# Hash attention and gated MLP: gaps in the buffers that VectorE reads bits from, and VectorE casts in parts of 7 and 5 stripes

## The chip, the core and the metric

The kernel runs on one core of a Trainium2 chip. Its time is the device time of one execution in microseconds (us), which is a little more than the span from the first to the last instruction in the profile. The engines are named as in the profile: PE is TensorE's matmuls and PEld its weight loads, DVE is VectorE, ACT is ScalarE, POOL is GpSimd and SP is SyncE; a "q" behind a name means the engine's queue. Durations of single instructions are in nanoseconds (ns).

## What is computed

Attention in which a query sees only keys of its own hash bucket, and a gated MLP behind it. Shapes: batch 4, heads 8, sequence 768, head size 64; 6 hash bits; the MLP has 3072 rows, width 512 and inner width 1536.

```python
q_bits = (np.einsum('bhsd,dk->bhsk', q, proj) > 0)      # 6 bits for each token
mask = q_bucket[:, :, :, None] == k_bucket[:, :, None, :]
scores = np.where(mask, scale * q @ k.T, -1e9)
attn = softmax(scores) @ v                               # then heads side by side: x (3072, 512)
g, val = x @ w_gate, x @ w_val
ffn_out = (gelu(g) * val) @ w_out
out = x + sigmoid(x @ w_res) * ffn_out
```

## The kernel before

**Tiles.** The 32 heads go in 16 pairs p (4 pairs for each batch element). For each pair and each side (q, k) the tokens lie in a tile `raw` of 128 partitions by 12 stripes of 64 floats: 6 stripes for each head of the pair. A second tile `nat` (6 of them in a ring, `nat_of`, 128 partitions by 12 stripes of 128 bf16) takes, in each stripe, the 64 values as bf16 (`cast`, L183 to L192), then 6 hash bits as plus or minus one half in columns 64 to 69, then a constant. So the product of a q and a k stripe contains the score and a large bonus for equal bits; a wrong bucket is driven to nothing by the exponential. `nat` is transposed into `aug`, in the first batch element by PE (`turn_pe`, evacuated by `turned`), later by DMA (`turn`).

**Bits.** There are three ways to them.
- `hash_mm`, `hash_tok`, `bits`: DVE transposes blocks of 32 by 32 (`tr`, L201), PE multiplies with the projection, DVE transposes the result back (`hash_tok`, L223) into a tile of 12 stripes of 32 floats, and four instructions (`bits`, L232) compare 32 partitions each with zero and write the bits into `nat`. For pairs 2 and 3 that tile is `ht` in SBUF; for the later batch elements it is `htp` in PSUM.
- `hash_heads`, `tok_heads` (L291), `bits_head` (L298): the same for pair 1, one head at a time, with a tile `hth` of 6 stripes in SBUF. Pair 0 uses `hash_one` and `bits_one`, in PSUM alone.
- `multiply` (L264, POOL), `add_up` (L271, DVE), `bits_val` (L275): for half of the later pairs POOL multiplies the tokens with the projection, DVE adds the products up into `hval` (tile hv, 12 stripes of 6 floats in SBUF), and one instruction on POOL or DVE compares.

**Stages.** `scores` makes two banks of scores with PE and one exponential of 128 x 1024 on ACT (L452); `values` multiplies the exponentials with v (L421); there are 9 such slots to a pair and 36 to a batch element. `finish` (L367, L368) normalizes into `x_tok`. After batch element b, `gate_val` runs the MLP's first half (L477 on PE, Gelu on ACT in L497, product on DVE in L499); its second half (`project`, L511 to L534) is spread between the attention slots of the next batch element.

**Order.** The schedule is manual: each engine executes its instructions in the order of the code. For the first batch element that order is written out by hand in the string ORDER, whose pieces are put up with `put`. The part that matters below reads:

```python
"scores 18, bits 3k, finish 10, vals_s 2, av 15, turn 2k1, ld 6q, evac 2q1, "
"scores 19, bits 3q, av 16, "
"scores 20, load_w 3, vals_a 3, evac 2k1, av 17, av 18, "
"scores 21, av 19, turn 3q0, "
"scores 22, turn 3k0, evac 3q0, "
```

WHO says which engine takes a piece: DVE casts 2k and 3k ("cast 2k", "cast 3k"), ACT casts 3q, POOL most of the others. Bits of a q side are compared on DVE, those of a k side on POOL and DVE by turns. For the later batch elements the tables FIRST and LATER give each piece a slot, and ON_ACT and ON_DVE an engine; `bits_val` is on DVE for two tiles of the second batch element and on POOL otherwise. The SP queue issues the loads and the DMA transposes, in order; POOL's queue issues the loads of the MLP's weights.

Of the kernel before, what the change touches and what calls it, by code (L numbers as in the profile page):

```python
# [9 lines left out]
FP32 = mybir.dt.float32  # L10
BF16 = mybir.dt.bfloat16
AF = mybir.ActivationFunctionType
ALU = mybir.AluOpType
# [4 lines left out]
def kernel(  # L18
# [12 lines left out]
    nc = tc.nc  # L31
    B, H, S, D = q.shape
    NBITS = proj.shape[1]
    DMODEL = H * D
    DFF = moe_w_gate.shape[1]
    P = 128
    KM = DMODEL // P
    KF = DFF // P
    T = S // P
    HP = H // 2  # L40
    NPAIR = B * HP
    HT = 2 * T
# [22 lines left out]
    hv_pool = ctx.enter_context(tc.tile_pool(name="hv", bufs=2))  # L65
    sm_pool = ctx.enter_context(tc.tile_pool(name="sm", bufs=2))
# [6 lines left out]
    raw, rawv, aug, vaug, vsums = {}, {}, {}, {}, {}  # L73
# [95 lines left out]
    for s in range(3):  # L169
        n = KF // 3  # L170
# [8 lines left out]
    def nat_of(x):  # L179
        return nat[(2 * x[0] + x[1]) % NN]  # L180

    def cast(p, side, eng, h0=0, h1=2):
        x = (p, side)  # L183
        scale = (1.0 / C) if side == 0 else 1.0
        sl = slice(h0 * T, h1 * T)
        dst = nat_of(x)[:, sl, 0:D]
        if eng is nc.scalar:
            nc.scalar.activation(dst, raw[x][:, sl], AF.Copy, scale=scale)
        elif side == 0:
            eng.tensor_scalar(dst, raw[x][:, sl], scale, 1.0, op0=ALU.mult, op1=ALU.mult)  # L190
        else:
            eng.tensor_copy(dst, raw[x][:, sl])  # L192

    t32, hsum, htok = {}, {}, {}
    TRING = (0, 1, 2, 0, 1, 2, None, None, 0, 1, None, None, 0, 1)
# [21 lines left out]
    def hash_tok(jobs, psum=False):  # L217
        n = 32 * len(jobs)
        if psum:
            ht = av_ps.tile([P, HT, 32], FP32, tag="av", name="htp")  # L220
        else:
            ht = sm_pool.tile([P, HT, 32], FP32, tag="ht", name="ht")
        nc.vector.transpose(ht[:n].rearrange("p c n -> p (c n)"),  # L223
                            hsum[jobs[0]][:n].rearrange("p c n -> p (c n)"))
        for j, x in enumerate(jobs):
            htok[x] = (ht, j)

    def bits(p, side, engs=(nc.vector,)):
        x = (p, side)
        ht, j = htok.pop(x)  # L230
        for a in range(4):
            engs[a % len(engs)].tensor_scalar(  # L232
                nat_of(x)[32 * a:32 * a + 32, :, D:D + NBITS],
                ht[32 * j:32 * j + 32, :, NBITS * a:NBITS * (a + 1)], 0.0, 0.5,
                op0=ALU.is_gt, op1=ALU.subtract)


# [17 lines left out]
    hval, prod = {}, {}  # L255
# [11 lines left out]

    def add_up(x, t):
        if x not in hval:
            hval[x] = hv_pool.tile([P, HT, NBITS], FP32, tag="hv", name="hv")  # L270
        nc.vector.tensor_reduce(hval[x][:, t:t + 2, :], prod.pop((x, t)),  # L271
                                axis=mybir.AxisListType.X, op=ALU.add)

    def bits_val(x, eng):
        eng.tensor_scalar(nat_of(x)[:, :, D:D + NBITS], hval.pop(x), 0.0, 0.5,  # L275
                                op0=ALU.is_gt, op1=ALU.subtract)


    def hash_heads(p, dh):
# [7 lines left out]
                             start=(dh == 0), stop=(dh == 1), tile_position=(0, 32 * j))  # L287

    def tok_heads(p):
        ht = sm_pool.tile([P, T, 32], FP32, tag="ht", name="hth")  # L290
        nc.vector.transpose(ht.rearrange("p c n -> p (c n)"),  # L291
                            hsum.pop(p).rearrange("p c n -> p (c n)"))
        htok[p] = ht

    def bits_head(p, side, hi, engs):
        j = 2 * hi + side
        for a in range(4):
            engs[a % len(engs)].tensor_scalar(  # L298
                nat_of((p, side))[32 * a:32 * a + 32, hi * T:hi * T + T, D:D + NBITS],
                htok[p][32 * j:32 * j + 32, :, NBITS * a:NBITS * (a + 1)], 0.0, 0.5,  # L300
                op0=ALU.is_gt, op1=ALU.subtract)

    def turn(p, side):
# [336 lines left out]
    def tokens(ps, psum=False):  # L640
        hash_tok([(p, side) for p in ps for side in range(2)], psum)
# [17 lines left out]
    for h in range(2):  # L659
        for e in range(2):  # L660
            x = "0%s%d" % ("qk"[e], h)
            put("tr " + x, lambda e=e, h=h: tr(0, e, h, h + 1))
            put("hash " + x, lambda e=e, h=h: hash_one(0, e, h, av_ps, "av"))
            put("cast " + x, lambda e=e, h=h, x=x: cast(0, e, WHO.get("cast " + x, G), h, h + 1))
            put("bits " + x, lambda e=e, h=h: bits_one(0, e, h))
            if x == "0q1":
                put("turn " + x, lambda: turn_pe(0, 0, 1, "av", av_ps))
            else:
                put("turn " + x, lambda e=e, h=h: turn_pe(0, e, h))
            if e == 0:  # L670
                put("evac " + x + "a", lambda h=h, x=x: turned(0, 0, h, WHO.get("evac " + x + "a", V), 0, 4))
                put("evac " + x + "b", lambda h=h, x=x: turned(0, 0, h, WHO.get("evac " + x + "b", V), 4, T))
            else:
                put("evac " + x + "a", lambda h=h, x=x: turned(0, 1, h, WHO.get("evac " + x + "a", V), 0, 2))
                put("evac " + x + "b", lambda h=h, x=x: turned(0, 1, h, WHO.get("evac " + x + "b", V), 2, T))
# [3 lines left out]
    for p in range(1, HP):  # L679
        for e in range(2):  # L680
            x = "%d%s" % (p, "qk"[e])
            put("tr " + x, lambda p=p, e=e: tr(p, e))
            put("cast " + x, lambda p=p, e=e, x=x: cast(p, e, WHO.get("cast " + x, G)))
            if p == 1:
                for h in range(2):
                    put("bits %s%d" % (x, h), lambda p=p, e=e, h=h, x=x: bits_head(p, e, h, WHO.get("bits %s%d" % (x, h), ((V,), (G, V))[e])))
            else:
                put("bits " + x, lambda p=p, e=e, x=x: bits(p, e, WHO.get("bits " + x, ((V,), (G, V))[e])))
            for h in range(2):
                y = "%s%d" % (x, h)  # L690
                put("turn " + y, lambda p=p, e=e, h=h, y=y: turn_pe(p, e, h, BANK[p][2 * h + e]))
                put("evac " + y, lambda p=p, e=e, h=h, y=y: turned(p, e, h, WHO.get("evac " + y, V)))
    for i in range(2):
        put("hash 1.%d" % i, lambda i=i: hash_heads(1, i))
    put("toks 1", lambda: tok_heads(1))
    for i in range(4):
        put("hash 2.%d" % i, lambda i=i: hashed((2, 3), i, i + 1))
# [17 lines left out]
    for b in range(B - 1):  # L715
        s0, p0 = b * NSLOT, (b + 1) * HP
        xs = [(p0 + i, side) for i in range(2) for side in range(2)]
        ys = [(p0 + 2 + i, side) for i in range(2) for side in range(2)]
        for j, (x, y) in enumerate(zip(xs, ys)):
            if b == 0:  # L720
                for z in (x, y):
                    n = "%d%s" % (z[0], "qk"[z[1]])
                    put("ld " + n, lambda z=z: load(*z))
                n = "%d%s" % (x[0], "qk"[x[1]])
                put("tr " + n, lambda x=x: tr(*x))
            else:
                place(b, "tr x", j, lambda x=x: tr(*x))
                place(b, "ld x", j, lambda x=x: load(*x))
                place(b, "ld y", j, lambda y=y: load(*y))
            place(b, "bits x", j, lambda x=x: bits(*x))  # L730
            place(b, "turn x", j, lambda x=x: turn(*x))
            place(b, "cast x", j, lambda x=x, e=who(b, "x%d" % j): cast(*x, e))
            place(b, "cast y", j, lambda y=y, e=who(b, "y%d" % j): cast(*y, e))
            place(b, "bits y", j, lambda y=y, e=who(b, "b%d" % j): bits_val(y, e))
            place(b, "turn y", j, lambda y=y: turn(*y))
            for t in range(T):
                place(b, "mul y%d" % j, t, lambda y=y, t=t: multiply(y, 2 * t))
                place(b, "add y%d" % j, t, lambda y=y, t=t: add_up(y, 2 * t))
        if b > 0:
            place(b, "hash", 0, lambda p0=p0: hashed((p0, p0 + 1)))  # L740
        place(b, "toks", 0, lambda p0=p0: tokens((p0, p0 + 1), True))
# [101 lines left out]
    for s in range(NSLOT - 1, LAST):  # L843
        p, c = divmod(s, NCH)
# [63 lines left out]
```

## Time and profile before

| | us |
|---|---|
| median of 3 runs | 342.3 |
| lowest and highest | 340.31, 344.82 |
| the profiled execution | 342.28 |
| its span | 340.6 |
| busy: PE, DVE, ACT, POOL | 328.7, 232.1, 221.7, 207.7 |
| first batch element's attention, until the Gelu table is loaded | 0 to 48.0 |
| first half of the MLP for it, until the next scores | to 81.8 |

A line of the timeline or of a list of instructions names the source line, the engine, the operation, the tile written and the tiles read, and the shapes as partitions x elements. In a list of instructions "x12: 185/194/2595" is the count and the shortest, the median and the longest duration in ns. A line of the waits names who waited for whom, and gives the total in us, the number of times and the longest. The granted clock of PE was 0.998 of full speed.

### The profile page before, as it was taken

What the parts mean: (1) busy time and instruction counts of PE and PEld (TensorE: products, weight loads), DVE (VectorE), ACT (ScalarE), POOL (GpSimd) and SP (SyncE); (2) the same over time, 40 slices, a digit from 0 to 9 for tenths busy, and PEclk for the clock granted to TensorE, in tenths of its full rate; (3) what the DMA queues carried; (4) which work ended last, traced back from release to release, by engine and by line L of the source; (5) the groups of instructions that cost most, each with busy time, mean ns of one, the idle gap of its engine ahead of it and who ended that gap; (6) DMA issues with size and microseconds to landing.
All of it is one profiled execution on the core that took longest, in us unless ns stands there. A gap on an engine that the chain in (4) does not pass through costs nothing.

```text
span 340.6 us, 7565 instructions
## 1 busy us (share of the span) xinstructions
PE 328.7 (97%) x2994; PEld 202.6 (60%) x3040; DVE 232.1 (68%) x422; ACT 221.7 (65%) x278; POOL 207.7 (61%) x236
## 2 busy tenths in 40 slices
PE   8997899999999999999999999999999999999995
PEld 5676665555666655565666665666566665566443
DVE  7899867998567877676777876776776344343343
ACT  5997984337999972345999992234999994223120
POOL 4899687899988682579989691579989000000000
PEclk9999999999999999999999999999999999999999
DMA  7989939799968350523996452502553331000012
GB/s 234 376 158 207 268 91 195 141 156 182 315 167 204 89 138 33 92 46 61 245 227 194 100 153 72 94 17 52 117 95 84 80 79 64 0 1 2 31 63 93
DMA packets 69827, 42.70 MB, mean 125 GB/s; under 512 B 47904, under 2 KB 66848, under 8 KB 69792
## 3 DMA queue, kind: packets, MB, share of 16 engines
q1 hardware_dynamic: 63376, 36.97, 43.4%
q0 software_dynamic: 6336, 5.24, 11.0%
q8 instruction: 24, 0.39, 0.5%
q14 instruction: 11, 0.09, 0.1%
q10 hardware_dynamic: 80, 0.00, 0.0%
HBM read 29.56 MB, written 6.29 MB: 105 GB/s over the span
## 4 chain that ended last, share of the span: by engine, by line
PE 88%; DVE 6%; issue 2%; ACT 2%; DMA 2%; DVEq 0%; ACTq 0%
PE sp L477 24%; PE fps L525 17%; PE sp L447 16%; PE av L421 9%; PE gvr L477 6%; PE rps L511 6%; PE gvf L477 3%; DMA x_sb<-x_tok 2%; PE hs L213 2%; ACT e L452 1%; DVE nat L232 1%; DVE hh L499 1%; PE pt L317 1%; DVE nat L135 1%; PE hs L242 1%
## 5 line engine op out<-in xcount | busy, mean ns | idle before, releaser
L264 POOL TENSOR_TENSOR pr<-ld,projt 128x768 f32<-128x768 f32 x72 | 129.8, 1816 | 46.2 <-DVE hv L271 45.1
L452 ACT ACTIVATE e<-sp 128x1024 bf16<-128x1024 f32 x144 | 142.6, 1027 | 8.1 <-PE sp L447 3.9
L447 PE MATMUL sp<-aug,aug 71*128 71x256 bf16 (+1 forms) x384 | 86.1, 325 | 1.6 <-ACT e L452 1.4
L525 PE MATMUL fps<-wo,hh 128*128 128x512 bf16 (+2 forms) x290 | 74.6, 361 | 1.1
L421 PEld LDWEIGHTS <-e 128*128 128x128 bf16 x1152 | 53.0, 97 | 29.1 <-issue 0.3
L271 DVE TENSOR_REDUCE hv<-pr 128x12 f32<-128x768 f32 x72 | 66.9, 936 | 3.3 <-POOL pr L264 3.2
L497 ACT ACTIVATE gt<-sp 128x768 bf16<-128x768 f32 x32 | 26.0, 811 | 55.6 <-PE sp L477 55.6
L421 PE MATMUL av<-va,e 128*128 128x65 bf16 x1152 | 57.7, 193 | 0.1
L499 DVE TENSOR_TENSOR hh<-gt,sp 128x768 bf16<-128x768 bf16 x36 | 34.3, 954 | 31.3 <-PE sp L477 29.6
L477 PE MATMUL sp<-x_sb,wv 128*128 128x256 bf16 (+1 forms) x277 | 52.3, 324 | 0.8 <-DVE hh L499 0.2
L477 PEld LDWEIGHTS <-wv 128*128 128x128 bf16 x384 | 37.5, 98 | 25.3 <-issue 0.7
L477 PEld LDWEIGHTS <-wg 128*128 128x128 bf16 x384 | 37.1, 98 | 25.2 <-issue 0.8
L477 PE MATMUL sp<-x_sb,wg 128*128 128x256 bf16 (+1 forms) x252 | 46.8, 325 | 0.3
L525 PEld LDWEIGHTS <-hh 128*128 128x128 bf16 x312 | 28.5, 97 | 22.1
L447 PEld LDWEIGHTS <-aug 71*128 71x128 bf16 x384 | 29.2, 97 | 12.0 <-issue 3.3
L529 DVE SCALAR_TENSOR_TENSOR fps<-th,fps 128x512 f32<-128x512 f32 (+2 forms) x26 | 17.0, 653 | 21.5 <-PE fps L525 20.1
L497 ACT ACTIVATE gt<-gvr 128x512 bf16<-128x512 f32 x16 | 9.6, 597 | 28.9 <-PE gvr L477 27.2
L511 PE MATMUL rps<-wr,x_sb 128*128 128x512 bf16 x90 | 26.4, 379 | 0.4
L515 ACT ACTIVATE th<-rps 128x512 f32<-128x512 f32 x24 | 14.2, 593 | 15.9 <-PE rps L511 15.6
L477 PE MATMUL gvr<-x_sb,wg 128*128 128x512 bf16 x61 | 20.9, 379 | 0.0
L201 DVE STREAM_TRANSPOSE t<-ld 128x768 f32<-128x768 f32 (+1 forms) x22 | 19.1, 883 | 0.0
L367 DVE RECIPROCAL rec<-av 128x6 f32<-128x6 f32 x32 | 6.2, 192 | 18.6 <-PE av L421 16.8
(83 smaller groups left out, 329.4 us busy)
## 6 DMA issues: line engine op xcount, KB each, us to landing
ldv<-in_v_dram SPq DMA_DIRECT2D x16, 384.0 KB, 5.4
out_dram<-o SPq DMA_DIRECT2D x23, 256.0 KB, 2.2
ld<-in_q_dram SPq DMA_DIRECT2D x15, 384.0 KB, 4.7
ld<-in_k_dram SPq DMA_DIRECT2D x15, 384.0 KB, 5.9
wg<-in_moe_w_gate_dram POOLq DMA_DIRECT2D x4, 384.0 KB, 5.7
wv<-in_moe_w_val_dram POOLq DMA_DIRECT2D x4, 384.0 KB, 6.9
wo<-in_moe_w_out_dram POOLq DMA_DIRECT2D x3, 512.0 KB, 6.8
wr<-in_moe_w_res_dram POOLq DMA_DIRECT2D x1, 512.0 KB, 5.7
```

Source lines behind the costliest of these rows:

```text
L201: nc.vector.transpose(t32[p, side][:, sl].rearrange("p c h n -> p (c h n)"), raw[p, side][:, sl].rearrange("p c d -> p (c d)"))
L264: nc.gpsimd.tensor_tensor(pr, raw[x][:, t:t + 2].unsqueeze(2).to_broadcast([P, 2, NBITS, D]), projt.unsqueeze(1).to_broadcast([P, 2, NBITS ...
L271: nc.vector.tensor_reduce(hval[x][:, t:t + 2, :], prod.pop((x, t)), axis=mybir.AxisListType.X, op=ALU.add)
L421: nc.tensor.matmul(av[p, hi][:, qt, :], e[:, off:off + P], va[:, hi, jt, 0:D + 1], start=first, stop=(p >= HP and jt == T - 1), skip_group ...
L447: nc.tensor.matmul(sp[:, off:off + nq * P], ks[0:KA, hi * T + jt, :], qs[0:KA, hi * T + qt0:hi * T + qt0 + nq, :], start=True, stop=True)
L452: nc.scalar.activation(e, sp, AF.Exp, scale=float(ALPHA))
L477: nc.tensor.matmul(o, w[:, kk, bass.ts(m, P)], xs[:, kk, c0:c1], start=(kk == 0), stop=(kk == KM - 1))
L497: nc.scalar.activation(gt[:, c0:c1], o, AF.Gelu)
L499: nc.vector.tensor_mul(hh[:, m, c0:c1], gt[:, c0:c1], o)
L511: nc.tensor.matmul(rps, x_sb[b][:, kk, t, :], wr[:, kk, :], start=(kk == 0), stop=(kk == KM - 1))
L525: nc.tensor.matmul(fps[:, cs], hh[:, m, bass.ts(t, P)], wo[:, m, cs], start=(m == 0), stop=(m == KF - 1))
L529: nc.vector.scalar_tensor_tensor(fps[:, cs], th[:, cs], 1.0, fps[:, cs], op0=ALU.add, op1=ALU.mult)
```

## The change

The tiles `ht`, `hth` and `hv` get room for one more stripe behind every third of their stripes (12 stripes become three groups of 4 with a gap of one stripe behind each; 6 become three groups of 2), and what writes and reads them uses patterns of three groups. The tile `htp` in PSUM stays as it was. A whole cast of a k side on DVE becomes two instructions, of 7 and of 5 stripes; casts of half a tile, casts on POOL and casts of a q side stay as they were.

```diff
+        elif eng is nc.vector and h1 - h0 == 2:
+            for c in (slice(0, 7), slice(7, HT)):
+                eng.tensor_copy(nat_of(x)[:, c, 0:D], raw[x][:, c])
         else:
             eng.tensor_copy(dst, raw[x][:, sl])
...
+    def gapped(n, w, name):
+        full = sm_pool.tile([P, 3, (n // 3 + 1) * w], FP32, tag=name[:2], name=name)
+        return full[:, :, 0:n // 3 * w]
...
-            ht = sm_pool.tile([P, HT, 32], FP32, tag="ht", name="ht")
-        nc.vector.transpose(ht[:n].rearrange("p c n -> p (c n)"),
-                            hsum[jobs[0]][:n].rearrange("p c n -> p (c n)"))
+            ht = gapped(HT, 32, "ht")
+        nc.vector.transpose(ht[:n].rearrange("p c n -> p (c n)") if psum else ht[:n],
+                            hsum[jobs[0]][:n].rearrange("p c n -> p (c n)") if psum else
+                            hsum[jobs[0]][:n].rearrange("p (u c) n -> p u (c n)", u=3))
...
-                ht[32 * j:32 * j + 32, :, NBITS * a:NBITS * (a + 1)], 0.0, 0.5,
+                ht[rows, :, cols] if len(ht.shape) == 3 and ht.shape[1] == HT else
+                ht[rows].rearrange("p u (c n) -> p u c n", n=32)[:, :, :, cols], 0.0, 0.5,
                 op0=ALU.is_gt, op1=ALU.subtract)
...
-            hval[x] = hv_pool.tile([P, HT, NBITS], FP32, tag="hv", name="hv")
-        nc.vector.tensor_reduce(hval[x][:, t:t + 2, :], prod.pop((x, t)),
+            hval[x] = hv_pool.tile([P, 3, HT // 3 + 1, NBITS], FP32, tag="hv", name="hv")
+        nc.vector.tensor_reduce(hval[x][:, t // 4, t % 4:t % 4 + 2, :], prod.pop((x, t)),
...
-        eng.tensor_scalar(nat_of(x)[:, :, D:D + NBITS], hval.pop(x), 0.0, 0.5,
-                                op0=ALU.is_gt, op1=ALU.subtract)
+        eng.tensor_scalar(nat_of(x)[:, :, D:D + NBITS], hval.pop(x)[:, :, 0:HT // 3], 0.0, 0.5,
+                          op0=ALU.is_gt, op1=ALU.subtract)
...
-        ht = sm_pool.tile([P, T, 32], FP32, tag="ht", name="hth")
-        nc.vector.transpose(ht.rearrange("p c n -> p (c n)"),
-                            hsum.pop(p).rearrange("p c n -> p (c n)"))
+        ht = gapped(T, 32, "hth")
+        nc.vector.transpose(ht, hsum.pop(p).rearrange("p (u c) n -> p u (c n)", u=3))
...
-                htok[p][32 * j:32 * j + 32, :, NBITS * a:NBITS * (a + 1)], 0.0, 0.5,
+                htok[p][32 * j:32 * j + 32].rearrange("p u (c n) -> p u c n", n=32)[
+                    :, :, :, NBITS * a:NBITS * (a + 1)], 0.0, 0.5,
                 op0=ALU.is_gt, op1=ALU.subtract)
```

## The prediction

> **What bounds the kernel now.** I read the engine shares first (PE busy for 328.7 of 340.6 us), then a table of busy time by stage, then the waits of the one stage in which PE is not full. From 45.1 to 315.8 us PE is busy for 267.9 of 270.7 us (the sum of its stage rows), so nothing that VectorE saves there can buy more than 2.8 us. The first 45 us are different:
>
> ```profile
> core 0: us, PE busy (x) PEld busy (x) DVE busy (x) ACT busy (x) POOL busy (x), PEclk, DMA share, GB/s
> 20.00:29.70 9.70, 9.70 (x155) 6.98 (x154) 8.91 (x23) 9.55 (x11) 9.01 (x17) 1.00 0.94 105
> 29.70:33.70 4.00, 1.98 (x36) 1.62 (x32) 3.92 (x6) 2.18 (x3) 3.84 (x9) 1.00 1.16 275
> 33.70:45.10 11.40, 10.16 (x145) 7.24 (x143) 8.61 (x15) 11.03 (x13) 7.90 (x9) 1.00 1.10 269
> 45.10:82.20 37.10, 36.51 (x277) 22.24 (x282) 31.51 (x55) 18.06 (x26) 33.23 (x26) 1.00 0.94 143
> ```
>
> The columns are the stretch, its length, and the busy time of PE, PEld, DVE, ACT and POOL. In the second row PE and ACT both lose about half of 4 us while DVE and POOL are full. ACT, with its exponentials, is what limits this part; its timeline shows one hole and no other between 9.4 and 47.9 us:
>
> ```profile
> 22.95 8.93 ACT L452 ACTIVATE e<-sp 128x1024 bf16<-128x1024 f32 x9
> 34.05 6.66 ACT L452 ACTIVATE e<-sp 128x1024 bf16<-128x1024 f32 x7 [2.17 <-PE sp L447]
> 40.56 0.86 ACT L188 ACTIVATE nat<-ld 128x768 bf16<-128x768 f32 x1
> 41.30 6.65 ACT L452 ACTIVATE e<-sp 128x1024 bf16<-128x1024 f32 x7
> ```
>
> The number in brackets is idle time and who ended it. The waits of 9 to 45 us say why PE was late, and the chain of waits names the instruction:
>
> ```profile
> ACT e L452 <- PE sp L447: 2.2, 1, 2.2
> PE pt L317 <- DVE aug L326: 2.0, 1, 2.0
> PEld L317 <- DVE nat L232: 1.6, 1, 1.6
> ...
> 29.79 2.60 DVE nat L232
> 32.41 0.56 DVE aug L326
> 33.02 0.49 PE pt L317 x6
> ```
>
> One TensorScalar that reads bits from ht took 2.60 us. The list of instructions on nat shows how far that is from its kind:
>
> ```profile
> L232 DVE TENSOR_SCALAR nat<-htp x48: 220/228/238, 54.4 to 235.9; 32x72 bf16<-32x72 f32 x48
> L232 DVE TENSOR_SCALAR nat<-ht x12: 185/194/2595, 24.4 to 29.8; 32x72 bf16<-32x72 f32 x12
> L298 DVE TENSOR_SCALAR nat<-hth x6: 171/175/211, 13.4 to 14.4; 32x36 bf16<-32x36 f32 x6
> L192 DVE CAST nat<-ld x2: 723/1216/1710, 20.3 to 21.4; 128x768 bf16<-128x768 f32 x2
> L275 DVE TENSOR_SCALAR nat<-hv x2: 198/928/1657, 69.1 to 85.0; 128x72 bf16<-128x72 f32 x2
> ```
>
> The three long maxima (2595, 1710, 1657 ns) sit on SBUF-to-SBUF TensorScalars and casts. The same operation from PSUM (htp) never leaves 220 to 238 ns in 48 instructions. While the 2595 ns one ran, POOL went back to back (a weight DMA issue 29.66 to 30.48, a cast to 31.33, a memset to 31.41, an addition to 32.32, next start 32.40), and DVE ended at 32.38, in that gap. The 1657 ns one ran from 69.09 to 70.75, and POOL's two DMA issues from 69.17 to 70.72. So these instructions wait for POOL to leave something that both need. Other DVE work beside POOL does not: the TENSOR_REDUCE of L271 reads SBUF 72 times beside 129.8 us of POOL multiplications and stays within 893 to 955 ns. The short instructions are also faster than their PSUM twins (194 against 228 ns for 72 elements), as if they read two halves at once; I take that second path to be what is fought over.
>
> **The change part by part.** The source in three groups and the destination in twelve stripes no longer divide alike into halves, so I expect the 12 ht, 6 hth and 2 hv instructions on DVE to run on one path, and not to wait.
>
> Bits, added: each ht one goes from 194 to about 228 ns (the htp row), 12 x 34 = 0.41 us; each hth one from 175 to 196 ns (the 36-element row of L250, from PSUM), 6 x 21 = 0.13; the two hv ones from 198 to about 232, 0.07. In all 0.6 us of DVE, at most 4 x 0.034 = 0.14 of it in the critical batch. It is hidden by ACT's queue; without that cover it costs those 0.14 us.
>
> Bits, removed: 2595 - 194 = 2.40 us at 29.79, 0.3 us in the two instructions before it (0.28 and 0.40 where 0.19 is normal), and 1657 - 198 = 1.46 us at 69.09.
>
> Casts: two become four. L201, SBUF to SBUF at 547 ns for 384 and 958 ns for 768 elements, gives 1.07 ns an element and 136 ns fixed, an estimate for one path: 0.62 us for 448 elements and 0.48 us for 320, 1.10 a cast, 2.20 for both, against 2.43 now. If the parts still take two paths, it is (0.38 + 0.31) x 2 = 1.38 plus their waits: none to 0.9 us each, about the mean POOL instruction there (0.65, 0.98, 0.84, 1.06), 1.38 to 4.98. I take 2.20. ACT is full from 9.4 to 31.9 us, so earlier casts buy nothing at the end; later ones cost only beyond the 0.6 us from the bits of 2q (about 25.2) to their PE turn at 25.78. [...]
>
> The transposes into gapped tiles (572 ns once, 384 ns once): between 0 and, by the 599 ns htp row, 0.03 us more each. POOL's own readers of the tiles (463 ns x4, 330 ns x10, 468 ns x10): the nearest bound for an awkward pattern is their own spread, 516, 346 and 482 at most, so 0 to 0.5 us over 24 instructions; POOL idles 45.1 us waiting for L271, so I take zero. The reductions into hv write the same 12 numbers. The change adds no wait and no DMA.
>
> What the end gains: without the wait, the last bits of 3q end at 30.0, the evacuation of 2k1 (0.54) at 30.5. PE finishes its values at 31.01 and goes straight on to the turn of 3q0 instead of waiting to 33.02; scores come at 31.35 and are done by about 31.95; ACT ends its earlier exponentials at 31.88. So ACT's hole shrinks from 2.17 to about 0.1: 2.1 us. ACT has no other hole to 47.95, so all of that reaches the MLP stage. There PE waits 0.24 us at 80.29 for a DVE product, which 1.4 us less DVE work at 69 may remove; I take 0.1 of 0 to 0.24. Late next is ACT itself. Sum: 342.28 - 2.1 - 0.1 = 340.1. The profiled execution (342.28, span 340.6) is at the median of the runs (342.3), so no correction.
>
> **Rivals.**
> The gain is lost to a transfer. The chain goes from a DMA of x_sb (33.69, 5.97 us) to ACT's queue at 39.66. If that landing stayed put, ACT's cast, due at 38.4, would wait 1.3 us and the gain be 0.9 or less, down to none if loads brought forward collide (DMA share 1.10 there): 341.4 to 342.3. Against: the queue's event lasts 17 ns, ACT never idles there, and the DMA starts on a product of DVE that moves forward too.
>
> The change does not do what it says: the bits still use both paths in spite of the gap. Then the wait stays where it is, and the time is 342.3. No row has unequal groups, so only the run can tell.
>
> Slower: the casts keep two paths, and four parts each meet POOL. Now two waits cost about 1.35 us (2.43 less two times 0.54). It decides when the parts' waits exceed 1.35 + 0.6 + 2.2 = 4.15 us together. Two of the longest kind (2.40) and two of 0.9 make 6.6, that is 2.5 us too late: 344.7. For it: POOL is full at 20 to 24 us. Against: single POOL instructions there are only 0.65 to 1.06 us. [...]
>
> More than forecast: the waits at 69 and in the casts also cost PE time that the in-order waits hide, the rest of the 0.59 us that PE loses from 45.1 to 82.2, and the hole at 29.79 was mild against other executions (the runs spread from 340.31 to 344.82): about 338.5.
>
> **How the numbers follow.** Forecast as worked out 0.62 (own range 339.2 to 341.2); lost to a transfer 0.13; nothing changes 0.10; slower 0.06; more 0.09. The predicted time is 340.1. From 338.0 to 342.8 all but the slower case lie inside, with some 0.5 us for the spread of runs. Two per cent is 6.8 us, about what a measurement of this kernel can tell from no change: the waits removed add up to 5.4 us of DVE time, so faster by over 2% needs something that I don't see (0.03); slower by over 2% takes nearly three times the worst cast case (0.03); within 2% is 0.94.
>
> **What would show it.** Right: nat<-ht maximum under 250 ns with its median near 228, nat<-hv on DVE near 232 both times, four casts of about 0.62 and 0.48 us, no hole of ACT near 32 us, PE's turn of 3q0 right behind the values. Wrong: ht medians still 194 with long maxima (the gap does nothing), cast parts of 0.4 us and scattered waits, or a new hole of ACT between 32 and 48 us, above all before L188. A time outside 338 to 342.8 with the hole gone would mean that the stages after 45 us moved for a reason not listed.

## The result and the profile after

| | before | after |
|---|---|---|
| median of 22 executions each, us | 344.0 | 340.4 |
| lowest and highest, us | 340.0, 346.14 | 339.24, 342.44 |
| the profiled execution and its span, us | 342.28, 340.6 | 340.34, 338.6 |

The ratio after to before is 0.9936, 95% interval 0.991 to 0.9962: 0.6% faster, clear of noise and within 2%. Ratios here leave out executions that are over 1.5% above the fastest of the same kernel, and in some sets below that drops many of the kernel before; where it matters, the medians of all executions stand beside them.

The instructions on nat that DVE executes, in the profile after (count, then shortest, median and longest ns):

```profile
L244 DVE TENSOR_SCALAR nat<-htp x48: 220/228/240, 52.7 to 234.1; 32x72 bf16<-32x72 f32 x48
L244 DVE TENSOR_SCALAR nat<-ht x12: 216/220/224, 24.7 to 30.1; 32x72 bf16<-32x72 f32 x12
L310 DVE TENSOR_SCALAR nat<-hth x6: 177/182/183, 13.9 to 14.8; 32x36 bf16<-32x36 f32 x6
L193 DVE CAST nat<-ld x4: 469/522/603, 20.8 to 22.7; 128x448 bf16<-128x448 f32 x2, 128x320 bf16<-128x320 f32 x2
L288 DVE TENSOR_SCALAR nat<-hv x2: 221/224/228, 67.4 to 83.1; 128x72 bf16<-128x72 f32 x2
```

No maximum stands out any more. The ht row has moved up to the row of its PSUM twin (220 against 228 ns), and the parts of a cast took 572 and 603 ns for 448 elements and 469 and 473 for 320, that is 0.80 and 1.02 ns for each element more, against the 1.07 ns that the prediction took for one path. "Two paths" and "one path" stand here and below for the faster and the slower duration of such an instruction (194 against 220 ns for 72 elements); that paths lie behind them is the prediction's reading and no profile shows it. That a long one waits for POOL is inferred as well, from where it ends: in the profile before, one at 32.38 us in POOL's gap from 32.32 to 32.40, and one at 70.75 us, 0.03 us behind two DMA issues of POOL. ACT's timeline of the same profile, from the cast of 3q on:

```profile
22.70 0.84 ACT L188 ACTIVATE nat<-ld 128x768 bf16<-128x768 f32 x1
23.43 15.58 ACT L465 ACTIVATE e<-sp 128x1024 bf16<-128x1024 f32 x16
38.87 0.86 ACT L188 ACTIVATE nat<-ld 128x768 bf16<-128x768 f32 x1
39.60 6.65 ACT L465 ACTIVATE e<-sp 128x1024 bf16<-128x1024 f32 x7
46.27 1.28 ACT L873 ACT_TABLE_LOAD   x1
```

The nine and seven exponentials with a hole of 2.17 us between them are now sixteen in a row. This execution's attention began 0.48 us later (first exponential at 9.90 instead of 9.42), so the Gelu table is loaded 1.70 us earlier by the clock (47.97 to 46.27) and 2.18 us earlier against the start. The span is 2.0 us shorter. In the MLP stage the one wait of PE for a product is still there, 0.34 us where it was 0.24:

```profile
40.70 0.59 PE L460 MATMUL sp<-aug,aug 71*128 71x256 bf16 x3 [0.80 <-ACT e L465]
43.45 0.59 PE L460 MATMUL sp<-aug,aug 71*128 71x256 bf16 x3 [0.23 <-ACT e L465]
78.49 1.46 PE L490 MATMUL sp<-x_sb,wv 128*128 128x512 bf16 x8 [0.34 <-DVE hh L512]
```

The numbers in brackets are PE's idle time before the group. The list of PE's waits in this profile has no other from 27 to 83 us (1.0 us for ACT in two, 0.3 us for DVE in one): the 2.02 us before the turn of 3q0 are gone, and up to the MLP stage ACT is what PE waits for.

### The profile page after: what moved, and what is told of

Read it like the earlier page. It is cut to its first block, busy times and chain, and to the rows that moved or that the text cites. A ratio compares the mean times of both kernels' runs of the same rounds, so it can differ in the third digit from the quotient of the medians.

```text
span 338.6 us, 7613 instructions
## 1 busy us (share of the span) xinstructions
PE 331.4 (98%) x3040; PEld 203.0 (60%) x3040; DVE 228.4 (67%) x424; ACT 221.7 (65%) x278; POOL 206.7 (61%) x236
## 4 chain that ended last, share of the span: by engine, by line
PE 90%; ACT 5%; DVE 3%; issue 1%; DVEq 0%; ACTq 0%
PE sp L490 25%; PE fps L538 18%; PE sp L460 16%; PE av L434 9%; PE gvr L490 7%; PE rps L524 6%; ACT e L465 5%; PE gvf L490 3%; PE hs L222 2%; PE hs L255 1%; DVE nat L135 1%; PE pt L330 1%; DVE hh L512 1%; PE pt L418 0%; DVE hv L284 0%
## 5 line engine op out<-in xcount | busy, mean ns | idle before, releaser
L538 PE MATMUL fps<-wo,hh 128*128 128x512 bf16 (+2 forms) x312 | 79.4, 362 | 0.0
L490 PE MATMUL sp<-x_sb,wv 128*128 128x512 bf16 (+1 forms) x288 | 52.8, 326 | 0.3 <-DVE hh L512 0.3
L490 PE MATMUL sp<-x_sb,wg 128*128 128x512 bf16 (+1 forms) x256 | 47.0, 326 | 0.0
L524 PE MATMUL rps<-wr,x_sb 128*128 128x512 bf16 x96 | 28.1, 379 | 0.0
L490 PE MATMUL gvr<-x_sb,wg 128*128 128x512 bf16 x64 | 21.7, 379 | 0.0
```

The costliest lines, as they stand in the source:

```text
L490: nc.tensor.matmul(o, w[:, kk, bass.ts(m, P)], xs[:, kk, c0:c1], start=(kk == 0), stop=(kk == KM - 1))
L524: nc.tensor.matmul(rps, x_sb[b][:, kk, t, :], wr[:, kk, :], start=(kk == 0), stop=(kk == KM - 1))
L538: nc.tensor.matmul(fps[:, cs], hh[:, m, bass.ts(t, P)], wo[:, m, cs], start=(m == 0), stop=(m == KF - 1))
```

## The experiments

Theory A is the prediction's: the gain is the one wait of the bits of 3q. Against it stand B (the sum of all waits removed on VectorE), C (the gap itself, not the uneven count) and, from what the first runs showed, D (the price of a hole in PE is more than its length). All kernels are timed beside the kernel before on the same chip.

**Only the gaps of ht.** The change without its casts, hth and hv:

```diff
+            ht = gapped(HT, 32, "ht")        # and its transpose and reader; nothing else of the change
```

> Only the tile ht has the gaps; hth, hv and the casts are as before. Theory A (the gain is the one wait of the bits of 3q, which is gone because three groups against twelve stripes do not split over two paths): ratio to the kernel before 0.993 to 0.994, no hole of ACT near 32 us, all twelve ht instructions on DVE between 215 and 225 ns, while the casts still have a wait (one over 1.2 us) and one hv instruction on DVE is still over 1.2 us. Theory B (the gain is the sum of all waits removed, 5 us of VectorE time in several places): this gives less than half of the gain, ratio 0.997 or more.

Measured: 340.55 us (339.69 to 340.92), ratio 0.9919 (0.9885 to 0.9953); before, 343.21 us. The ht instructions are at 216/219/223 ns and ACT has no hole. In the same profile the casts and hv still wait:

```profile
L192 DVE CAST nat<-ld x2: 716/1217/1718, 21.0 to 22.1; 128x768 bf16<-128x768 f32 x2
L285 DVE TENSOR_SCALAR nat<-hv x2: 198/918/1637, 67.6 to 83.5; 128x72 bf16<-128x72 f32 x2
```

So the whole gain comes with ht alone, and waits of 1.4 us at 67 us and 1.2 us at 22 us cost nothing that can be measured. Theory B falls.

**All but the gaps of ht.**

```diff
-            ht = gapped(HT, 32, "ht")
+            ht = sm_pool.tile([P, HT, 32], FP32, tag="ht", name="ht")
```

> The complement: hth and hv have the gaps and the casts are in parts of 7 and 5, but ht is as before. Theory A: the wait of one ht instruction stays (over 1.5 us), ACT keeps a hole of 1.5 to 2.2 us near 32 us, ratio 0.998 to 1.002. Theory B: more than half of the gain is here, ratio 0.995 to 0.997. If the casts in parts only moved VectorE by some 0.3 us against POOL, the ht wait may meet another POOL instruction and be of another length; then ACT's hole goes with it.

Measured: 345.57 us (341.83 to 346.5), ratio 1.0061 (1.0022 to 1.0101). That is 0.6% slower than the kernel before, which no theory had said. The wait is there (2420 ns, in the four of the second line below), and a second one that the profile of before does not have: the two ht instructions at 27.65 us took 1.25 us together (before: 0.40 us, at 27.20 us). Together they make PE's hole 2.55 us where it was 2.02, but the price is larger than this length. DVE's and PE's timelines in this profile, and the stages behind the hole:

```profile
27.65 1.25 DVE L243 TENSOR_SCALAR nat<-ht 32x72 bf16<-32x72 f32 x2
30.17 3.19 DVE L243 TENSOR_SCALAR nat<-ht 32x72 bf16<-32x72 f32 x4
31.05 0.41 PE L433 MATMUL av<-va,e 128*128 128x65 bf16 x8
34.00 0.80 PE L329 MATMUL pt<-ident,nat 128*71 128x128 bf16 x6 [2.55 <-DVE aug L338]
34.60 1.06 PE L459 MATMUL sp<-aug,aug 71*128 71x256 bf16 x3
```

```profile
33.00:35.00 2.00, 1.00 (x8) 1.02 (x9) 1.66 (x6) 0.00 (x0) 1.84 (x5) 0.52 1.19 272
35.00:37.00 2.00, 2.00 (x13) 1.31 (x11) 1.01 (x2) 1.02 (x1) 1.54 (x5) 0.50 1.19 266
37.00:39.00 2.00, 2.00 (x19) 1.45 (x18) 0.73 (x2) 1.02 (x1) 0.14 (x1) 0.50 1.33 188
39.00:41.00 2.00, 2.00 (x31) 1.56 (x30) 1.59 (x4) 1.32 (x2) 2.00 (x2) 0.77 1.19 220
```

The third number from the right is the granted clock of PE. It is at a half behind the hole: 0.52, 0.50, 0.50 and 0.77 over 2 us each are 6.8 us at 0.50 and the rest at 1.00. The same six transposes take 0.80 instead of 0.50 us and three scores 1.06 instead of 0.60, and ACT, which waits for scores, has holes of 3.42, 0.47, 0.91 and 0.50 us instead of one. The page of before shows clock 9 in all its slices: its profiled execution had a hole of 2.02 us and kept the clock.

**Only the casts in parts.**

```diff
+            for c in (slice(0, 7), slice(7, HT)):
+                eng.tensor_copy(nat_of(x)[:, c, 0:D], raw[x][:, c])
```

> The casts of 2k and 3k in parts of 7 and 5 stripes, all tiles without gaps. Theory A: ratio 0.998 to 1.002; the four parts take 0.60 and 0.47 us (one path, no waits), the ht wait and ACT's hole stay. The rival that the casts are what makes VectorE late for the bits of 3q: the ht wait is gone and the ratio is 0.994. The slower case of the prediction (parts on two paths, each waiting): parts of 0.4 us with waits and a ratio over 1.003.

Measured: 345.25 us (340.71 to 346.58), ratio 1.004 (0.9991 to 1.0089). The profiled execution is the odd one out of 12, at 340.71 us. It has no wait over 0.2 us in the ht instructions and the casts (hv still waits, 1637 ns at 67.7 us):

```profile
L235 DVE TENSOR_SCALAR nat<-ht x12: 184/191/356, 24.2 to 29.7; 32x72 bf16<-32x72 f32 x12
L193 DVE CAST nat<-ld x4: 470/523/605, 20.3 to 22.2; 128x448 bf16<-128x448 f32 x2, 128x320 bf16<-128x320 f32 x2
```

So the wait of 3q comes in some executions and not in others. Here the last comparison of 3q started at 29.68, 0.09 us into POOL's weight-DMA issue (29.59), and went through in 191 ns; in the kernel before it started at 29.79, 0.13 us into that issue (29.66), and took 2595. All the other 11 executions lie at 343.67 us or above. The parts run on one path without waits (470 to 605 ns), as expected, but with them the bad meeting seems likelier; that they do it by shifting DVE against POOL is not shown.

**Gaps behind halves instead of thirds.**

```diff
-        full = sm_pool.tile([P, 3, (n // 3 + 1) * w], FP32, tag=name[:2], name=name)
-        return full[:, :, 0:n // 3 * w]
+        full = sm_pool.tile([P, 2, (n // 2 + 1) * w], FP32, tag=name[:2], name=name)
+        return full[:, :, 0:n // 2 * w]
```

> As the changed kernel, with a gap behind every half of the stripes instead of every third: two groups of six (two of three in hth), so the counts on both sides are even. Theory A (the odd count is what matters): the ht instructions are back at about 190 ns median, one waits for more than 1.5 us, ACT's hole is back, ratio 0.998 to 1.002. Theory C (the gap itself, another address of the stripes, is what matters): 215 to 225 ns, no wait, ratio 0.994.

Measured: 345.24 us (341.56 to 346.6 in 11 executions, and one of 406.74 us at clock 0.80 that is far outside all others), ratio 1.0063 (1.0018 to 1.0108). The profile has the wait back:

```profile
L244 DVE TENSOR_SCALAR nat<-ht x12: 185/206/2414, 24.2 to 32.7; 32x72 bf16<-32x72 f32 x12
L310 DVE TENSOR_SCALAR nat<-hth x6: 172/174/255, 13.4 to 14.4; 32x36 bf16<-32x36 f32 x6
```

Gaps behind halves left the ht instructions as they are without gaps (median 206 ns, as in the run of all but the gaps of ht, and one of 2414), gaps behind thirds gave 220 ns and no wait. Theory C falls.

**Casts of 6 and 6 stripes**, a single execution, with all else as changed:

```diff
-            for c in (slice(0, 7), slice(7, HT)):
+            for c in (slice(0, 6), slice(6, HT)):
```

> As the changed kernel, with the casts in parts of 6 and 6 stripes instead of 7 and 5. If an even count brings the two paths back: the parts take about 0.36 us without a wait (136 ns and half of 384 elements at 1.07 ns), and at least one of the four waits for POOL and takes over 0.6 us. If parts alone are enough: all four take 0.55 us (384 elements on one path). Either way ACT is full there, so the time is that of the changed kernel within the spread, 338 to 342 us.

Measured: 341.13 us.

```profile
L193 DVE CAST nat<-ld x4: 315/346/350, 20.7 to 21.9; 128x384 bf16<-128x384 f32 x4
```

Two paths are back, near the expected 0.36 us for 384 elements, but none of the four waited (350 ns at most): that half of the expectation missed. In this profile PE waits once, 0.7 us, for bits that POOL compares, which it does not in the profile after, and ACT has a hole of 0.86 us ahead of the exponentials at 28.20 us; what made POOL late is not shown.

**All hv comparisons on DVE, without and with gaps.**

```diff
-    ON_DVE = ((0, "b0"), (0, "b2"))
+    ON_DVE = tuple((b, "b%d" % j) for b in range(2) for j in range(4))
```

> As the kernel before, but all twelve comparisons of hv tiles are on VectorE (before: two of twelve, POOL the other ten). Theory: in the stages after 45 us PE is full and VectorE's waits cost next to nothing, so several of the twelve take over 1 us (POOL's multiplications last 1.8 us) and the time is within 0.4% of the kernel before. Rival: a wait of VectorE holds up the products and copies behind it in order and PE with them; then 10 more waits of about 1 us cost 3 to 10 us, ratio 1.01 to 1.03.

> As the changed kernel, with all twelve comparisons of hv tiles on VectorE. All twelve take 220 to 230 ns. Theory that the wait matters only where ACT runs dry: ratio 0.993 to 0.996 to the kernel before, about the same distance from the run without the gaps as the change itself. Rival that waits after 45 us cost: the distance to the run without gaps is larger than the change's 0.6%, by as much as that one lost.

Measured without gaps: 343.67 us (341.67 to 346.81), ratio 1.0044 (1.0004 to 1.0084); with gaps: 340.26 us (339.13 to 341.14), 0.9967 (0.9939 to 0.9995); before, 342.26 us. The twelve took 188/198/1634 ns (with gaps 210/217/229): the longest waited and at least half did not, where several of over 1 us had been expected, so it is not shown that much of a dose was given, and this says little about waits after 45 us. Up to 45 us this kernel without gaps is the kernel before, and its profile (of an execution of 346.81 us) shows there what the one without the gaps of ht showed: two ht instructions near 28 us that took 1.27 us together, one of 2424 ns, a PE hole of 2.57 us, and the half clock behind it for 6.8 us (0.82, 0.50, 0.50, 0.50 and 0.97 over the 2 us stretches from 33 us on).

**The changed kernel again, and DVE's lateness put back as plain work.** Since the clock was at 0.50 behind PE holes of 2.55 and 2.57 us, the last question was the price of a hole of given length, with nothing contended. Transposes of 3q are repeated ahead of its bits (the same data are written again; the longest transpose from raw took 969 ns in the profile before and in the one after, with medians of 963 and 962 ns, PE's hole grows by 1.01 us with each one more, and the ht instructions behind them took 216 to 224 ns, so all of these are taken to wait for nothing):

```diff
-        "scores 19, bits 3q, av 16, "
+        "scores 19, delay, bits 3q, av 16, "
...
+    put("delay", lambda: [tr(3, 0) for _ in range(2)])      # 2, 3 or 4
```

> The changed kernel once more, as the base of the three runs beside it: 340.0 to 340.8 us, executions within about 2 us of each other, ratio to the kernel before 0.990 to 0.997. If the spread of the kernel before (339.8 to 346.2 us) comes from the ht wait, it is gone here; if it comes from elsewhere, it is here too.

> The changed kernel with two more transposes of 3q on VectorE (0.89 us each, the same data written again) just ahead of the bits of 3q: the wait put back as plain work of 1.8 us, with nothing contended. About 0.45 us of it is slack, so PE's hole is 1.3 us and ACT's 1.4. Theory D (the price of VectorE's lateness is ACT's hole, and more than that only if PE's hole is long enough to lower its clock): 341.8 us, all executions within 2 us, granted clock 1.00 behind the hole.

> As delay2 with three transposes, 2.7 us: PE's hole 2.2 us. Theory D: executions in two groups or more, about 342.6 us where the clock holds and 344 to 346 us where it falls to a half for some microseconds behind the hole. Rival (lateness costs its own length and nothing else): one group at 342.6 us.

> As delay2 with four transposes, 3.6 us: PE's hole 3.1 us. Theory D: nearly all executions lose the clock, 346 to 347.5 us, with a granted clock near 0.5 for about 5 us behind the hole. Rival (lateness costs its own length): 343.5 us and the clock as before.

| | PE's hole in its profile, us | median, us | executions, us |
|---|---|---|---|
| changed again | none | 340.6 | 339.74 to 340.94 in 8 of 10; 342.3, 342.81 |
| 2 transposes | 1.40 | 341.45 | 340.87 to 341.75 in 8 of 10; 343.05, 344.73 |
| 3 transposes | 2.41 | 343.83 | 342.3 to 342.67 in 4 of 10; 343.56 to 346.54 in 6 |
| 4 transposes | 3.42 | 345.04 | 344.98 to 346.08 in all 4 |

With three transposes, the executions of the first group have a granted clock of 0.998 to 0.999 over the span and the six others of 0.990 to 0.995: same code, same work, two prices. With four, all have 0.989 to 0.995. The stages behind the hole, with three (a profile from the first group) and with four:

```profile
33.00:35.00 2.00, 1.46 (x18) 1.26 (x19) 1.81 (x5) 0.43 (x1) 1.84 (x5) 1.00 1.19 274
35.00:37.00 2.00, 2.00 (x39) 1.65 (x37) 1.53 (x3) 2.00 (x3) 1.22 (x4) 1.00 1.26 242
```

```profile
33.00:35.00 2.00, 0.59 (x8) 0.63 (x9) 1.90 (x7) 0.00 (x0) 0.36 (x3) 0.93 1.19 281
35.00:37.00 2.00, 2.00 (x12) 1.34 (x11) 1.12 (x3) 1.02 (x1) 1.84 (x5) 0.50 1.17 272
37.00:39.00 2.00, 2.00 (x31) 1.69 (x30) 0.67 (x3) 1.16 (x2) 0.76 (x2) 0.71 1.24 250
```

Theory D holds, and its rival falls: by length alone, four transposes should have given 343.5 us and three one group. The sizes were off: with four, 346 to 347.5 us and some 5 us of half clock were expected, and with two, two of the ten executions fell out of the one group. The half clock lasted 0.28 + 2 + 1.16 = 3.4 us here and 6.8 us in the profile without the gaps of ht.

In this set the ratio of the changed kernel to the one before is 1.001 (0.9975 to 1.0044), with medians of all executions of 340.6 and 344.37 us. It is no contradiction: 12 of the 25 executions of the kernel before lay over 344.5 us here, which is 1.5% above their fastest, and ten of the other 13 belong to the two fastest of the four groups described below.

**The cast of 4q on POOL**, on top of the change:

```diff
-    ON_ACT = ((0, "x0"), (0, "x2"), (0, "y0"), ...
+    ON_ACT = ((0, "x2"), (0, "y0"), ...
```

> As the changed kernel, with the cast of 4q on POOL instead of ACT. In the changed kernel ACT runs without a hole to 46.3 us, so it is now the limit of the first part; this cast is 0.86 us of it at 38.9, and behind it PE waits 0.80 us for an exponential. POOL waits 1.39 us for a load at 36.6 to 38.0, where the cast fits. If ACT is the limit: 0.7 to 0.9 us less than the changed kernel, ratio to the kernel before 0.990 to 0.993. If something else is close behind (PE, or the transfers), less than 0.3 us.

Measured: 339.83 us (339.42 to 340.55), ratio 0.995 (0.9926 to 0.9973), before 342.26 us; the changed kernel was not in this set, the nearest to it (all hv on DVE, with gaps) had 340.26 us.

```profile
22.64 0.84 ACT L188 ACTIVATE nat<-ld 128x768 bf16<-128x768 f32 x1
23.38 22.30 ACT L465 ACTIVATE e<-sp 128x1024 bf16<-128x1024 f32 x23
45.69 1.28 ACT L873 ACT_TABLE_LOAD   x1
```

ACT runs 23 exponentials in a row and is 0.53 us earlier against the start of its row (0.58 less 0.05); the span is 338.2 instead of 338.6 us. Some of the expected 0.7 to 0.9 us is lost to the next waits (PE now waits 0.38 us at 47.9 for x_tok). The intervals of this and of the change overlap, so it is the lowest median of the study and not a shown gain.

## Why the prediction was right, and what it had wrong

**The 86 executions of the kernel before that ran beside the experiments** tell what was removed. They fall into four groups by time, and the clock goes with them:

| time, us | executions | mean time | mean granted clock |
|---|---|---|---|
| 339.4 to 341.1 | 26 | 340.3 | 0.999 |
| 341.5 to 342.9 | 20 | 342.2 | 0.998 |
| 343.5 to 344.8 | 21 | 344.3 | 0.994 |
| 345.3 to 346.2 | 19 | 345.7 | 0.990 |

By the profiles, the first is an execution without a long wait of an ht instruction (as in the profile of the casts in parts, at 340.71), and the second has the one at 29.8 us and keeps the clock (the profile shown before, at 342.28). Three more profiles have two waits of ht instructions, two that take 1.25 to 1.27 us together near 28 us (0.40 in the profile before) and one of 2.4 us near 30 us, a PE hole of 2.54 to 2.57 us and a half clock behind it: gaps behind halves, at 343.78 us with 3.4 us of half clock, would be of the third group; the kernel without the gaps of ht, at 346.15 us, and all hv on DVE without gaps, at 346.81 us, both with 6.8 us, of the fourth or just above it. A half clock for 3.4 us and for 6.8 us takes 0.5 x 3.4 / 342 = 0.005 and 0.010 off the mean clock, which is what the groups show. That the groups have these causes is inferred from these profiles and from the delays; of the kernel before itself only the second group was profiled. Three executions of the first group, at 340.83 to 341.12 us, have a clock of 0.994, so a lower clock is not always this dear. Of 63 executions with the gaps of ht (the changed kernel twice, ht only, all hv on DVE, the cast on POOL), 58 lie at or below 341.3 us and none above 342.81.

Point by point:
- *The bits go to one path and do not wait.* Right: 220, 182 and 224 ns for predicted 228, 196 and 232, no maximum above 228. That unequal groups would do it was a guess, since no row of the profile before had any; the run with halves (median 206 ns, one of 2414) shows that it takes the thirds.
- *The casts.* One path, 572 and 603, and 469 and 473 ns, for predicted 0.62 and 0.48 us; the other estimate, 0.38 and 0.31 us on two paths, is not met. Nothing of before showed that 7 or 5 stripes would go to one path: that was the author's choice between the two estimates. Parts of 6 and 6 did not (315 to 350 ns for 384 elements); why is not shown.
- *Earlier or later casts cost nothing.* Wrong in the odds. With the casts in parts and two-path bits, 1 of 35 executions (all but ht, casts only, halves without the disturbed one) was below 341.3 us, against 26 of 86 before. The casts cost nothing where they stand, but the kernels with them lose more often; why is not shown. That they are in the change has no measured worth once ht is uneven (340.55 us without them).
- *The hole is worth 2.1 us.* Right for the profiled execution (2.18 us against the start), wrong as a price. It was one of four: 0, 1.9, 4.0 and 5.4 us above the first group. The 86 executions have a mean of 342.9 us, 2.6 above the first group, so a prediction from one profile came out right by luck, because that profile lay near the middle. That it was at the median was read from three runs; over 22 the median is 344.0 us, and between the medians of all executions the change is worth 3.6 us. The spread of the runs, 340.31 to 344.82, was in the prediction, as a remark in the rival of more; it should have been a term.
- *0.1 us from the wait at 69 us.* Nothing: the wait is gone (221 to 228 ns) and PE's wait at 78.49 is 0.34 us.
- *Rivals.* Nothing was lost to the transfer of x_sb: ACT goes through the cast of 4q at 38.87 without a hole. The casts did not wait. That the hole was mild against other executions was right, for reasons not named: a second wait, and the clock.

What stays open: what makes a hole cost the clock (2.02 and 2.41 us kept it in their profiles, 2.54 to 2.57 us lost it in three, and of the ten executions with three transposes four kept it and six did not); why the half clock lasted 3.4 us in two profiles and 6.8 us in two; what shifts POOL against DVE from one execution to the next (the first exponential starts at 9.42 and 9.90 us in the two profiles shown), and why a few executions of the changed kernel (3 of 22, 341.96 to 342.44 us, and one at 342.81 when it ran again) have a mean clock of 0.990 as well; no profile fell into one of them.

## What to carry to other kernels

The wait of this kernel was paid in odds (26 of 86 executions were without its price): before pricing one from a profile, look at the spread and the granted clock of all executions, and ask whether the profiled one is the typical one. A hole in PE of about 2.4 us had two prices here, its length and, in 6 of 10 executions, the clock behind it, while waits of 1.2 and 1.4 us in casts and hv cost nothing that could be measured: here the waits to remove first were those that leave PE empty, whatever their share of the busy time. The slower form of an instruction gave the faster kernel: 26 ns more for each of twelve instructions (194 to 220 ns) took away a wait that, by the four groups, cost 1.9 to 5.4 us in 60 of 86 executions.

## What the runs showed of the hardware

- DVE's TensorScalar from ht to nat (32 x 72) took a median of 191 to 206 ns with 12 stripes against 12 or 2 groups against 12, and of 219 to 220 ns with 3 groups against 12. A cast of 384 elements in 6 stripes took 315 to 350 ns, casts of 448 and 320 elements in 7 and 5 stripes 572 to 603 and 469 to 473 ns. Long ones, up to 2595 ns, were among the ungapped and the halved ones and the casts of 12 stripes alone; with 3 groups the longest ht instruction took 225 ns and the longest hv instruction 229, and the longest cast of 7 stripes took 610 ns.
- In two profiles, 0.04 us lay between the two outcomes: an ht instruction that started 0.09 us into a POOL weight-DMA issue took 191 ns, and one at 0.13 us 2595. In two other profiles a group of four that began 0.29 us into one had one of 2420 or 2414 ns. It is no rule: the hv instruction of 69.09 us took 1657 ns over two such issues, the first of which began 0.08 us after it.
- PE holes of 1.40 and 2.02 us kept the clock at 1.00 in their profiles, one of 2.41 us kept it in one profile while 6 of 10 executions of that kernel had a mean clock of 0.990 to 0.995, holes of 2.54 to 2.57 us were followed by a clock of 0.50 in three profiles, for 3.4 us (one) and 6.8 us (two), and one of 3.42 us in its profile, for 3.4 us.
